# A planner that takes transfers to land later, early weight sums on GpSimd alone, half loads for unused half blocks, and another order of first-layer products

## The chip, the cores and the metric

The kernel runs on one core of a Trainium2 chip. The metric is the time of one execution on the device in microseconds (us), the median of several executions. The engines of the core are TensorE (PE in the profile; its weight loads are PEld), VectorE (DVE), ScalarE (ACT), GpSimd (POOL) and SyncE (SP, which issues the transfers). Matrix products are written to PSUM[...]; everything else lies in SBUF or in device memory.

## The reference

Two parts follow each other. The first is a state-space scan (batch 4, 8 heads, 768 steps, head size 32, state size 16, in chunks):

```python
L = np.exp(cum[:, :, :, None] - cum[:, :, None, :]) * causal
M = np.einsum('bhin,bhjn->bhij', Cc, Bc) * L
y = np.einsum('bhij,bhjd->bhid', M, xc) + np.einsum('bhin,bhnd->bhid', Cc, state) * np.exp(cum)[..., None]
state = decay_full[:, :, None, None] * state + np.sum(Bx, axis=2)
```

The second takes its result as x with 3,072 tokens of 256 numbers and runs four experts (256 to 1,024 to 256, all fp32), each weighted per token:

```python
p = domain_probs / (domain_probs.sum(-1, keepdims=True) + 1e-09)
for e in range(E):
    h = np.maximum(x @ w1[e], 0.0)
    out += p[:, e:e + 1] * (h @ w2[e])
```

## The kernel before

The tokens are 24 chunks of 128. They are taken in five blocks: three of four chunks (scheme `B`) and two of six (scheme `H`). For each block the scan of its chunks gives the tokens, and then both layers of all four experts are run on them. Each expert's 1,024 hidden columns are four blocks of 256 (`fb`), so there are 16 of them.

The products of a block are not made one by one. A scheme is a fast matrix multiplication: it forms sums of weight blocks and sums of token blocks, makes fewer products of 128 x 256 blocks, and recovers the wanted blocks from sums of the products. `B` takes 2 x 2 x 2 blocks with 7 products, `H` takes 3 x 2 x 3 blocks with 15. One call of `product` (line 831) is one such product. `Scheme.sums` lists the sums of weights, ten for `H` and four for `B` in each layer; `Scheme.blocks` says which blocks come straight from the weights. Blocks called "b" enter sums alone, and never a product by themselves.

`operands` loads the weights of one group into W tiles (32 of them, 128 x 512), makes the sums (line 942) into further W tiles and stores these in device memory (`w_d`, line 947). Where a group's sums are already stored, it loads them instead (line 939). For the `H` blocks, which come last, the sums are made early, during units 1 to 10, by `early_sums`, with a due time that lies a unit later. A unit is a step of the main loop: in scheme `B` two groups of two weight blocks, in scheme `H` one group of three. Its first-layer products (`twos_first`, `threes_first`) are interleaved by `put` with the second-layer products (`visit`) of the unit before.

In `threes_first`, `mul(r)` makes product r into a bank, `snap` copies a bank into a V tile (ScalarE, line 840), `seed` copies a V tile into a bank for further accumulation (ScalarE, line 845), `combine` adds or subtracts (VectorE or GpSimd, line 858), `gate` applies the rectifier and the expert's share (VectorE, line 866). `visit` copies its bank out on line 1111. The scan part has `mask` (ScalarE, line 437, from an xb tile), `scan` (VectorE, line 456), `fade` (GpSimd, line 462), the products of line 444 (scores), 469 and 775 (outputs), copies of the outputs (ScalarE, lines 791, 476 to 479), and `cts` (GpSimd, line 739).

The order of work on each engine is not written out by hand, except TensorE's: `Plan.run` is a list scheduler. Every piece of work has a price in us per engine it may run on, pieces that it needs, and the tiles that it touches. The scheduler walks through a modelled time and takes, for the engine that is free first, the ready piece with the earliest latest time (`latest`, counted back from its consumers or from a due time). TensorE takes its pieces in the given order. A transfer is modelled with a rate of 310 KB per us and fixed lags. A piece that needs the result of another may start `HOP` = 0.2 us after it, and a tile may be taken 0.2 us after its last use. Work with two engines in its price (`B256`, `B512`) goes to GpSimd only if that is in time and VectorE has a backlog. The resulting orders are then issued; on the chip each engine works through its own in order, held by semaphores.

`BY_DMA` is empty, so `sums_by_dma` is never called.

Of the kernel before, what the change touches and what calls it, by code (L numbers as in the profile page):

```python
# [10 lines left out]
ALU = mybir.AluOpType  # L11
# [7 lines left out]
HOP = 0.2  # L19
# [5 lines left out]
EARLY = 1, 2, 3, 4, 5, 6, 7, 8, 9, 10  # L25
SOFT = 1
ROUND = 0, 3, 2, 0, 4
RATE = 310.0
BY_DMA = ()
AFTER = 1  # L30
HELD = ("x", "w"), (5, 8), (0, 7)
LAST = (0, 1), (0, 2), (1, 1), (1, 2), (0, 0), (1, 0)
LATE = (13, 2), (6, 9), (11, 4), (10, 12), (3,), (1, 14), ("x", "w"), (5, 8), (0, 7)
ACC = 5.0
PAIRS_AT = {(3, 2): {0: 0, 1: 1}, (4, 2): {0: 0, 2: 1}, (4, 3): {0: 0, 1: 1, 2: 2},
            (6, 3): {0: 0, 2: 1, 3: 2}}


class Home:
    def __init__(self, tile_):  # L40
        self.tile, self.free, self.full = tile_, 0.0, False


class Value:
# [18 lines left out]
class Plan:  # L63
# [61 lines left out]
    def homed(self, w, at):  # L125

        taken, when = {}, at
        for v in w.touched:
            if v.home is not None:
                continue  # L130
            if w.reuse and w.reuse.left == 1 and w.reuse.kind == v.kind:
                taken[v] = w.reuse.home
                when = max(when, w.reuse.end)
                continue
            spare = [h for h in self.spare[v.kind] if h not in taken.values()]
            if v.seeded:
                spare = [h for h in spare if h.full]
            elif v.kind == "bank":
                hollow = [h for h in spare if not h.full and h.free <= at]
                spare = hollow or spare  # L140
            if not spare:
                return None, None
            if v.kind == "bank" and len(self.spare["bank"]) <= sum(
                    x.home is None and x.place < v.place for x in self.banks):
                return None, None
            if v.kind == "V" and len(spare) <= KEEP and w.latest + self.late > at + 8:
                return None, None
            if v.kind == "W" and len(spare) <= sum(
                    x.home is None and x.latest < v.latest for x in self.ws):
                return None, None  # L150
            h = min(spare, key=lambda h: h.free)
            taken[v] = h
            when = max(when, h.free + HOP)
        return when, taken

    def backlog(self, queue, now, free, but):
# [8 lines left out]
    def run(self, line, at, begin):  # L165
# [18 lines left out]
        while todo:  # L184
# [4 lines left out]
            for w in waiting[e]:  # L189
                if w.start is not None or e == "PE" and w.place != head:  # L190
                    continue
                ready = max([w.ready, w.after.nominal + late if w.after else 0.0] + [
                    n.end + (0.0 if n.by == e and e != "SP" else HOP) for n in w.needs])
                if len(w.on) > 1 and e == "POOL":
                    if max(ready, now) + w.on[e] > w.latest + late + SLACK or self.backlog(
                            waiting["DVE"], now, t["DVE"], w) < BACK:
                        continue
                rank = w.latest
                if e == "DVE" and w.two and self.port > now + 0.05:
                    rank += YIELD  # L200
                if best is not None and ready <= now and rank >= best[0]:
                    continue
                when, homes = self.homed(
                    w, max(now, ready, self.port if e == "POOL" and w.port else 0.0))
                if when is None:
                    continue
                if when <= now + 0.02:
                    if best is None or rank < best[0]:
                        if e == "DVE" and w.two:
                            when = max(when, self.port)  # L210
                        best = rank, w, when, homes
                elif soon is None or when < soon:
                    soon = when
# [30 lines left out]
            for v in w.touched:  # L244
                v.left -= 1
                v.end = max(v.end, w.end)
                if v.left == 0 and not (w.reuse is v and any(
                        x.home is v.home for x in w.touched if x is not v)):
                    v.home.free, v.home.full = v.end, v.fills
                    self.spare[v.kind].append(v.home)  # L250
# [58 lines left out]
def kernel(  # L309
# [55 lines left out]
    def some(n, shape, name, pool=const):  # L365
# [16 lines left out]
        "M": some(6, [HN, NQ, D], "M"),  # L382
        "gate": some(3, [P, max(b.n for b in blocks), P], "gate"),
        "Y": some(12, [P, FB], "Y"),
        "dram": [None] * 200,
    }
    st = {c: {} for c in range(NCH)}
    one = nc.const_aps.tensor(1.0, [P, 1])
# [495 lines left out]
            return w1[e, i * P:i * P + P, f * FB:f * FB + FB]  # L884
        return w2[e, f * FB:f * FB + FB, i * P:i * P + P].rearrange("(j p) m -> p j m", p=P)

    def sums_by_dma(scheme, fbs, l, after, due):

        slot = {}
        for i, pair in enumerate(scheme.shared[l]):  # L890
            d = stored_sums((*fbs, l, i))
            for j, r in enumerate(pair):
                slot[r] = d[:, j * FB:j * FB + FB]
        sums = {}
        for n, (r, x, y, sign) in enumerate(scheme.sums):
            if x not in scheme.blocks[l]:
                x, y = y, x
            f, i = scheme.blocks[l][x]
            v = sums[r] = value("dram")
            split = (lambda t: t) if l == 1 else (lambda t: t.rearrange("p (j m) -> p j m", j=JJ))  # L900
            dma(lambda e, r=r, f=f, i=i: nc.sync.dma_start(
                out=split(slot[r]), in_=source(fbs[f], l, i)), 1, 300, writes=[v], due=due, after=after)
            if y in sums:
                plan.add({"POOL": 1.0}, lambda e, r=r, y=y: nc.gpsimd.dma_start(
                    out=slot[r], in_=slot[y], accum_op=ALU.add), port=False, lag=ACC, kb=300,
                    reads=[sums[y]], part=[v], due=due, after=after)
            else:
                g, h = scheme.blocks[l][y]
                plan.add({"POOL": 1.0}, lambda e, r=r, g=g, h=h: nc.gpsimd.dma_start(
                    out=split(slot[r]), in_=source(fbs[g], l, h), accum_op=ALU.add), port=False, kb=300,  # L910
                    lag=ACC, part=[v], due=due, after=after, reads=[v])

    def operands(k, scheme, fbs, l, after=None, due=None):

        load, half = ((load_w1, w1_half), (load_w2, w2_half))[l - 1]
        where = {}
        for f, fb in enumerate(fbs):
            v = value("W")
            if l == 1 and f == 1 and (*fbs, l, 0) in w_d:
                dma(lambda e, v=v, fb=fb: nc.sync.dma_start(  # L920
                    out=v.t[:, FB:], in_=w1_rows(fb, 1)), kb=128, part=[v], after=after)
            else:
                dma(lambda e, v=v, fb=fb: load(fb, v.t), part=[v], after=after)
            for r, x in scheme.blocks[l].items():
                if x[0] == f:
                    where[r] = v, x[1]
# [10 lines left out]
        if keys[0] in w_d:  # L937
            for key, v in zip(keys, shared):
                dma(lambda e, v=v, key=key: nc.sync.dma_start(out=v.t, in_=w_d[key]), part=[v])
        else:  # L940
            for r, x, y, sign in scheme.sums:
                plan.add(B256, lambda e, r=r, x=x, y=y, sign=sign: (  # L942
                    on(e).tensor_add if sign > 0 else on(e).tensor_sub)(view(r), view(x), view(y)),
                    two=True, reads=[where[x][0], where[y][0]], part=[where[r][0]])
            for key, v in zip(keys, shared):
                d = stored_sums(key)
                dma(lambda e, v=v, d=d: nc.sync.dma_start(out=d, in_=v.t), reads=[v],
                    due=due or (lambda v=v: v.readers[-1]))
        weights[k, fbs, l] = where, view

    def early_sums(scheme, fbs, l, after, due):
        operands("early", scheme, fbs, l, after, due)

    def token_sums(k):
        Y, scheme = {}, blocks[k].scheme
# [72 lines left out]
    def threes_first(k, fbs):  # L1028
# [11 lines left out]
        mul(11, b7)  # L1040
        a12 = combine(b7, s12, -1)
        gate(2, 0, mul(0, seed(s7)))
        b6 = mul(6)
        t67 = combine(snap(b6), s7, -1)
        b3 = mul(3)
        s3 = snap(b3)
        b5 = mul(5, seed(a12))
        gate(2, 2, b5)
        mul(2, b7)
        gate(1, 2, combine(b7, s12, -1))  # L1050
        mul(10, b3)
        v = combine(b3, s12, -1)
        t67 = combine(t67, v)
        mul(14, b6)
        f = combine(b6, a12)
        f = combine(f, b5, -1)
        z02 = combine(f, s3, -1, reuse=s3)
        gate(0, 2, z02)
        mul(13, b7)
        gate(1, 0, b7)  # L1060
        b8 = mul(8, seed(v))
        gate(0, 1, b8)
        u = combine(f, b8, -1)
        gate(1, 1, mul(4, seed(v)))
        mul(1, b8)
        gate(2, 1, negate(t67, b8))
        gate(0, 0, mul(9, seed(u)))
        return seq, h
# [247 lines left out]
    for u, (k, groups) in enumerate(units):  # L1316
# [21 lines left out]
            leave(*ending, due=lambda n=u + AFTER: ends[min(n, len(ends) - 1)])  # L1338
            ending = None
        for _ in range(EARLY.count(u)):  # L1340
            (sums_by_dma if len(early) in BY_DMA else early_sums)(
                H, *early.pop(0), merged[0],
                lambda n=u + SOFT: ends[min(n, len(ends) - 1)])
        if groups is None:
            behind = second(k, *held, HELD if k == len(blocks) - 1 else (), plain)
        else:
# [80 lines left out]
```

## Time and profile before

| what | value |
|---|---|
| time, median of 3 runs | 635.5 us (634.72 to 637.93) |
| the profiled execution's own time | 636.7 us |
| its span (first to last instruction) | 634.9 us |
| granted TensorE clock | 0.998 |
| busy PE / DVE / ACT / POOL | 624.9 / 530.3 / 261.4 / 204.6 us |
| transfers on the main queue | 127.46 MB, 62.8% of 16 engines' span |
| full and half loads of raw weights (w<-in_w_dram) | 149 of 256 KB, 19 of 128 KB |
| sums of weights, line 942 | 80 on DVE, 84 on POOL |

A line of the timeline gives the start in us from the beginning of the span, the length in us, the engine, the line of the kernel, the operation, result and operands, the number of instructions merged, and in brackets the idle time of the engine just before and what ended it. A line of the waits gives who waited for whom, the total in us, how often, and the longest. DMA issues stand on SPq and are not counted as busy time of an engine; a semaphore event of a transfer is its landing.

### The profile page before, as it was taken

To read this page: it belongs to the slowest core of one execution; us is meant where nothing else is said; L and a number is where in the kernel's file an instruction comes from. 1 tells how busy PE (TensorE), PEld (TensorE's weight loads), DVE (VectorE), ACT (ScalarE), POOL (GpSimd) and SP (SyncE) were. 2 spreads that over 40 slices of the span, in tenths; PEclk is the share of its full clock that TensorE was granted. 3 is DMA by queue.
4 is the path that set the end of the run, shared out by engine and by line. 5 is a ranking of instruction groups with operands and counts; after the bars stand their busy time and mean duration, and the time that the engine had idled before them with its cause. 6 is when DMAs were issued, how large, how long until landed. Compare 5 with 4: busy or idle time off the path is not lost.

```text
span 634.9 us, 10197 instructions
## 1 busy us (share of the span) xinstructions
PE 624.9 (98%) x3363; PEld 528.7 (83%) x3363; DVE 530.3 (84%) x915; ACT 261.4 (41%) x538; POOL 204.6 (32%) x221
## 2 busy tenths in 40 slices
PE   9899999999998999999999999999999999999997
PEld 5687788888886888888888888888888888888886
DVE  7889987988968887888978887979897887779784
ACT  4123543434344253434434335455434235455441
POOL 4252533445422255442424614301053600101010
PEclk9999999999999999999999999999999999999999
DMA  6999794595899658489999928455232324951001
GB/s 202 287 303 362 234 323 160 175 299 141 275 322 341 233 172 268 107 256 305 326 349 363 305 40 294 150 154 174 77 91 83 101 45 120 377 167 56 2 1 51
DMA packets 110933, 128.37 MB, mean 202 GB/s; under 512 B 28692, under 2 KB 76832, under 8 KB 110880
## 3 DMA queue, kind: packets, MB, share of 16 engines
q1 hardware_dynamic: 110500, 127.46, 62.8%
q8 instruction: 27, 0.44, 0.3%
q10 hardware_dynamic: 380, 0.25, 0.1%
q14 instruction: 26, 0.21, 0.1%
HBM read 102.79 MB, written 24.89 MB: 201 GB/s over the span
## 4 chain that ended last, share of the span: by engine, by line
PE 51%; DVE 1%; issue 0%; DVEq 0%
PE bank L831 50%; PE bank L444 1%; PE bank L469 0%; DVE LT L456 0%; DVE v L866 0%; PE bank L775 0%; PE bank L1234 0%; DVE bank L1016 0%; DVE v L858 0%; DVE v L1162 0%; DVE v L1239 0%; DVE w L942 0%; DVEq L1239 0%
## 5 line engine op out<-in xcount | busy, mean ns | idle before, releaser
L831 PE MATMUL bank<-v,w 128*128 128x256 f32 x1864 | 441.6, 381 | 4.8 <-ACT A L479 2.4
L831 PEld LDWEIGHTS bank<-v,w 128*128 128x128 f32 x1864 | 351.2, 190 | 61.5 <-DVE v L866 5.4
L831 PE MATMUL bank<-Y,w 128*128 128x256 f32 x792 | 203.1, 379 | 0.1
L858 DVE TENSOR_TENSOR v<-v,v 128x512 f32<-128x512 f32 x216 | 161.9, 769 | 12.2 <-ACT v L840 8.1
L831 PEld LDWEIGHTS bank<-Y,w 128*128 128x128 f32 x792 | 150.2, 190 | 21.3 <-issue 0.7
L866 DVE SCALAR_TENSOR_TENSOR v<-bank,gate 128x512 f32<-128x512 f32 x172 | 116.7, 684 | 40.6 <-PE bank L831 33.5
L858 POOL TENSOR_TENSOR v<-v,v 128x512 f32<-128x512 f32 x54 | 79.7, 1480 | 214.1 <-DVE v L866 167.6
L1111 ACT COPY v<-bank 128x512 f32<-128x512 f32 x107 | 62.6, 585 | 157.6 <-PE bank L831 157.0
L845 ACT COPY bank<-v 128x512 f32<-128x512 f32 (+1 forms) x192 | 107.4, 577 | 33.0 <-DVE v L858 21.4
L840 ACT COPY v<-bank 128x512 f32<-128x512 f32 x106 | 62.0, 586 | 100.6 <-PE bank L831 87.4
L942 POOL TENSOR_TENSOR w<-w,w 128x256 f32<-128x256 f32 x69 | 58.1, 855 | 75.2 <-DMA w<-in_w_dram 23.6
L456 DVE TENSOR_TENSOR_SCAN LT<-ab,ident 128x512 f32<-128x512 f32 x42 | 54.3, 1311 | 3.7 <-DMA ab<-acut_d 3.7
L858 DVE TENSOR_TENSOR v<-bank,v 128x512 f32<-128x512 f32 x40 | 27.4, 685 | 11.8 <-PE bank L831 11.5
L942 DVE TENSOR_TENSOR w<-w,w 128x256 f32<-128x256 f32 x69 | 31.6, 487 | 6.3 <-DMA w_d<-w 3.8
L601 DVE TENSOR_TENSOR MT<-bank,LT 128x256 f32<-128x256 f32 x93 | 32.1, 410 | 0.2
L739 POOL TENSOR_TENSOR cts<-ctm,dec 128x256 f32<-128x256 f32 x20 | 17.1, 865 | 43.0 <-DVE dec L736 32.1
L437 ACT ACTIVATE ctm<-xb,tmask 128x128 f32<-128x128 f32 x48 | 16.0, 394 | 36.1 <-DMA xb<-in_xbc_dram 18.1
L1162 POOL TENSOR_TENSOR v<-v,v 128x256 f32<-128x256 f32 x22 | 18.9, 875 | 34.0 <-ACT v L1111 32.7
L462 POOL TENSOR_TENSOR MT<-xb,LT 128x128 f32<-128x128 f32 x20 | 11.5, 579 | 31.6 <-DVE LT L456 20.6
L1162 DVE TENSOR_TENSOR v<-v,v 128x256 f32<-128x256 f32 x38 | 17.2, 482 | 3.0 <-ACT v L1111 2.7
L942 POOL TENSOR_TENSOR w<-w 128x256 f32<-128x256 f32 x15 | 13.2, 885 | 16.3 <-DMA w<-in_w_dram 14.8
L1016 DVE TENSOR_TENSOR bank<-bank,v 128x512 f32<-128x512 f32 x22 | 15.2, 690 | 1.8 <-PE bank L831 1.8
(76 smaller groups left out, 210.5 us busy)
## 6 DMA issues: line engine op xcount, KB each, us to landing
w<-in_w_dram SPq DMA_DIRECT2D x149, 256.0 KB
w<-w_d SPq DMA_DIRECT2D x130, 256.0 KB
w_d<-w SPq DMA_DIRECT2D x82, 256.0 KB
ab<-acut_d SPq DMA_DIRECT2D x21, 512.0 KB
xb<-in_xbc_dram SPq DMA_DIRECT2D x12, 320.0 KB
gate<-p_d SPq DMA_DIRECT2D x10, 384.0 KB
gate<-p_d SPq DMA_DIRECT2D x11, 256.0 KB
w<-in_w_dram SPq DMA_DIRECT2D x19, 128.0 KB
```

Source lines behind the costliest of these rows:

```text
L437: nc.scalar.mul(ctm[:, t], xb[:, OCT:OCT + P], tmask[:, t:t + 1])
L456: nc.vector.tensor_tensor_scan(out=LT.rearrange("p h s -> p (h s)")[:, lo:lo + w], data0=src, data1=ident.rearrange("p h s -> p (h s)")[:, ...
L601: nc.vector.tensor_mul(MT[:, h, 0:P], g, LT[:, h])
L739: plan.add({"POOL": .78}, lambda e: nc.gpsimd.tensor_mul(s["cts"].t, s["ctm"].t, s["dec"].t.unsqueeze(1).to_broadcast([HN, NT, P])), reads ...
L831: nc.tensor.matmul(out=o, lhsT=w[:, j], rhs=x if half is None else x[:, j], start=(start and j == 0), stop=(j == 1), skip_group_check=True)
L840: act(.6, lambda e: nc.scalar.copy(out=flat(v), in_=bank.t), reads=[bank], writes=[v])
L845: act(.6 if to > FB else .38, lambda e: nc.scalar.copy(out=bank.t[:, :to], in_=flat(v)[:, :to]), reads=[v], writes=[bank])
L858: plan.add(engines, lambda e: (on(e).tensor_add if sign > 0 else on(e).tensor_sub)(flat(v), whole(x), whole(y)), reads=[x, y], writes=[v], ...
L866: dve(.7 if x.kind == "bank" else .74, lambda e: nc.vector.scalar_tensor_tensor(out=h.t, in0=whole(x).rearrange("p (j m) -> p j m", j=JJ), ...
L942: plan.add(B256, lambda e, r=r, x=x, y=y, sign=sign: (on(e).tensor_add if sign > 0 else on(e).tensor_sub)(view(r), view(x), view(y)), two= ...
L1111: act(.6, lambda e: nc.scalar.copy(out=flat(v), in_=bank.t), reads=[bank], writes=[v])
L1162: plan.add(engines, lambda e: (on(e).tensor_add if sign > 0 else on(e).tensor_sub)(o[1](), x[1](), y[1]()), reads=[v for v in vs if v is n ...
```

## The change

Five things are altered. A constant `MARGIN` of 4.0 us takes the place of `HOP` where a piece that does not run on SP needs the result of a transfer, and where such a piece takes a tile that was last touched by a transfer. The sums with a due time, which are the early ones, may run on GpSimd alone. `operands` loads only the used half of a weight tile where exactly one of its two blocks enters a product and the sums are stored already; before, it did so for the first layer's second tile only. `threes_first` makes its products in another order. The unused code of sums by transfers goes, and `operands` is called directly.

```diff
-RATE = 310.0
-BY_DMA = ()
+RATE, MARGIN = 310.0, 4.0
...
-        self.tile, self.free, self.full = tile_, 0.0, False
+        self.tile, self.free, self.full, self.dma = tile_, 0.0, False, False
...
-            when = max(when, h.free + HOP)
+            when = max(when, h.free + (MARGIN if h.dma and "SP" not in w.on else HOP))
...
-                    n.end + (0.0 if n.by == e and e != "SP" else HOP) for n in w.needs])
+                    n.end + (MARGIN if n.kb and e != "SP" else 0.0 if n.by == e and not n.kb else HOP)
+                    for n in w.needs])
...
             for v in w.touched:
                 v.left -= 1
                 v.end = max(v.end, w.end)
+                v.home.dma = w.kb > 0 if w.end == v.end else v.home.dma
...
-            if l == 1 and f == 1 and (*fbs, l, 0) in w_d:
-                dma(lambda e, v=v, fb=fb: nc.sync.dma_start(
-                    out=v.t[:, FB:], in_=w1_rows(fb, 1)), kb=128, part=[v], after=after)
+            used = {x[1] for r, x in scheme.blocks[l].items() if x[0] == f and r != "b"}
+            if len(used) == 1 and (*fbs, l, 0) in w_d:
+                i, = used
+                dma(lambda e, v=v, fb=fb, i=i: nc.sync.dma_start(
+                    out=half(v.t, i), in_=source(fb, l, i).rearrange(
+                        "p (j f) -> p j f", j=JJ) if l == 1 else source(fb, l, i)),
+                    kb=128, part=[v], after=after)
...
-                plan.add(B256, lambda e, r=r, x=x, y=y, sign=sign: (
+                plan.add({"POOL": .78} if due else B256, lambda e, r=r, x=x, y=y, sign=sign: (
...
         gate(2, 0, mul(0, seed(s7)))
-        b6 = mul(6)
-        t67 = combine(snap(b6), s7, -1)
         b3 = mul(3)
         s3 = snap(b3)
         b5 = mul(5, seed(a12))
         gate(2, 2, b5)
+        mul(10, b3)
+        v = combine(b3, s12, -1)
+        b6 = mul(6)
+        t67 = combine(snap(b6), s7, -1)
         mul(2, b7)
         gate(1, 2, combine(b7, s12, -1))
-        mul(10, b3)
-        v = combine(b3, s12, -1)
-        t67 = combine(t67, v)
         mul(14, b6)
...
         gate(0, 2, z02)
-        mul(13, b7)
-        gate(1, 0, b7)
+        gate(1, 1, mul(4, seed(v)))
         b8 = mul(8, seed(v))
         gate(0, 1, b8)
         u = combine(f, b8, -1)
-        gate(1, 1, mul(4, seed(v)))
+        mul(13, b7)
+        gate(1, 0, b7)
         mul(1, b8)
+        t67 = combine(t67, v)
         gate(2, 1, negate(t67, b8))
         gate(0, 0, mul(9, seed(u)))
...
-            (sums_by_dma if len(early) in BY_DMA else early_sums)(
-                H, *early.pop(0), merged[0],
-                lambda n=u + SOFT: ends[min(n, len(ends) - 1)])
+            operands("early", H, *early.pop(0), merged[0],
+                     lambda n=u + SOFT: ends[min(n, len(ends) - 1)])
```

More of the change, by code (lines that the diff above doesn't have):

```diff
@@ L33 @@
 LATE = (13, 2), (6, 9), (11, 4), (10, 12), (3,), (1, 14), ("x", "w"), (5, 8), (0, 7)
-ACC = 5.0
 PAIRS_AT = {(3, 2): {0: 0, 1: 1}, (4, 2): {0: 0, 2: 1}, (4, 3): {0: 0, 1: 1, 2: 2},
@@ L384 @@
         "Y": some(12, [P, FB], "Y"),
-        "dram": [None] * 200,
     }
@@ L885, in source @@
         return w2[e, f * FB:f * FB + FB, i * P:i * P + P].rearrange("(j p) m -> p j m", p=P)
[L887 to L911, printed above, removed]
     def operands(k, scheme, fbs, l, after=None, due=None):
@@ L949, in operands @@
         weights[k, fbs, l] = where, view
-    def early_sums(scheme, fbs, l, after, due):
-        operands("early", scheme, fbs, l, after, due)
     def token_sums(k):
```

## The prediction

> **What bounds the kernel now.** I read the page first, then the waits of TensorE, then the timeline around each of them. On the page, the busy line and the slices:
>
> ```profile
> PE 624.9 (98%) x3363; PEld 528.7 (83%) x3363; DVE 530.3 (84%) x915; ACT 261.4 (41%) x538; POOL 204.6 (32%) x221
> ...
> PE   9899999999998999999999999999999999999997
> ...
> DMA  6999794595899658489999928455232324951001
> ```
>
> TensorE is busy 624.9 of 634.9 us, and the chain that ended last is nearly all L831. The number of products (`product`, L831) does not change, so the change can win only what TensorE stands still: 10.0 us, of which the ends (a start-up that is not planned, 1.1 us, and the last copy and store, 3.7 us) are out of reach. The dips are in slices 2 and 13. From the waits of PE:
>
> ```profile
> PE bank L831 <- ACT A L479: 2.4, 1, 2.4
> PE bank L831 <- DVE v L866: 2.0, 2, 1.2
> ...
> PE bank L831 <- DVE v L858: 0.4, 2, 0.2
> ```
>
> Five waits, 4.8 us. The timeline shows how the largest came about:
>
> ```profile
> 18.64 0.71 PE L444 MATMUL bank<-ctm,xb 32*128 32x256 f32 x8
> ...
> 22.56 0.69 ACT L437 ACTIVATE ctm<-xb,tmask 128x128 f32<-128x128 f32 x2 [7.72 <-DMA xb<-in_xbc_dram]
> ...
> 23.16 0.35 ACT L791 COPY v<-bank 128x256 f32<-128x256 f32 x1
> 23.41 0.18 ACT L479 COPY A<-bank 128x32 f32<-128x32 f32 x1
> ...
> 23.64 1.99 PE L831 MATMUL bank<-v,w 128*128 128x256 f32 x8 [2.37 <-ACT A L479]
> ```
>
> ScalarE stood 7.7 us at `mask` (L437), whose xb had not landed. Behind it in ScalarE's order stood the copies that empty a bank (L791, L479); their matmuls were over at 18.7. TensorE wanted that bank and waited 2.4 us. The planner had believed the transfer landed earlier. The second place:
>
> ```profile
> 188.03 0.42 DVE L942 TENSOR_TENSOR w<-w,w 128x256 f32<-128x256 f32 x1 [2.90 <-DMA w_d<-w]
> ...
> 192.36 1.99 PE L831 MATMUL bank<-v,w 128*128 128x256 f32 x8 [1.24 <-DVE v L866]
> 193.25 1.22 DVE L942 TENSOR_TENSOR w<-w,w 128x256 f32<-128x256 f32 x3 [0.94 <-DMA w_d<-w]
> ...
> 195.13 4.58 PE L831 MATMUL bank<-v,w 128*128 128x256 f32 x20 [0.77 <-DVE v L866]
> ...
> 199.88 1.13 PE L831 MATMUL bank<-v,w 128*128 128x256 f32 x4 [0.17 <-DVE v L858]
> ```
>
> Here VectorE stood 2.9 and 0.9 us at an early sum of weights (L942), because the W tile it was to write was still being stored (w_d<-w). The gatings (L866) and sums (L858) queued behind came late, and TensorE waited 1.24 + 0.77 + 0.17 = 2.18 us.
>
> [...] In the trace L858 with a PSUM input takes 685 ns, from SBUF alone 769 on average; L942 on VectorE takes 406 ns at least and up to 1,472. [...] the trace has 855 against 487 ns.
>
> **The change part by part.**
>
> 1. *Later landings (MARGIN 4.0 instead of HOP 0.2).* No instruction is added or taken away; the order on ACT, DVE, POOL and SP changes, TensorE's does not through this part. Anything that reads a transfer, or writes a tile last touched by one, is placed 3.8 us later in the plan. At 23.64, the mask goes behind L791 and L479, which can then run from 18.7 on: 2.4 us of idle go (2.8 by the weight loads' own idle time). What is late next there is VectorE: its L601 ends at 22.1, before TensorE would reach outputs([3]) at some 22.7, so no new wait. At 67.18 ScalarE waits 5.83 us in the same way; TensorE's weight load loses 0.5 us at 68.46, and I count 0.3. Sum of this part: 2.7 us. Behind the new delays stand `scores` (needs ctm), `cts` and `fade` on POOL (need xb, ah). The tightest `cts` of the trace starts at 172.8 for an L775 at 179.6, 6.1 us ahead after its 0.73; the others are 12 to 24 us ahead. 3.8 us later fits. Where TensorE in the plan now has to wait for weights, its real order stays, but filler may get in front of work it needs: one filler is 0.7 to 1.2 us (L858, L456).
>
> 2. *Early sums on GpSimd alone.* There are 100 (5 groups, 2 layers, 10 sums). The line's view from 136 us on, where only these are left:
>
> ```profile
> L942 POOL TENSOR_TENSOR w<-w,w x41: 718/735/1639, 135.9 to 334.9; 128x256 f32<-128x256 f32 x41
> L942 DVE TENSOR_TENSOR w<-w,w x31: 407/417/1472, 151.4 to 337.1; 128x256 f32<-128x256 f32 x31
> ```
>
> With the other form (w<-w) VectorE makes 35 there, POOL 46. Moved: 35 x 0.487 = 17 us less on VectorE, 35 x 0.855 = 30 us more on POOL over 200 us, where POOL is about a third busy: it has the room. VectorE then never stands at the store of a W tile: the 2.18 us of 192 to 200 go, and I count 1.9, as gatings there also had L456 scans of 1.2 us ahead of them. POOL still meets such waits (4.3 us at 177.83), with `fade`, `cts` and some L858 queued behind. [...] At 306.91 (0.23 us idle) VectorE also had sums ahead: 0.2.
>
> 3. *Half blocks.* Layer 1 already loads half of group block 1. New are halves for layer 2 (block 0 of scheme B, block 1 of scheme H). If these are as many as the 19 halves of now, 19 x 131 KB = 2.5 MB of 128 MB go, 2%; at 62.8% of 634.9 us for 127.46 MB that is 8 us of the 16 engines' time. TensorE waits for no weights beyond 0.3 us, so it is worth nothing directly: a transfer hidden anyway. It makes landings slightly earlier; from 0 to 0.5 us, I take 0. Issues stay the same number. Their rows are 512 bytes instead of 1,024[...].
>
> 4. *Order in `threes_first`.* Ten units, all from some 340 us on, where no wait of TensorE is seen at all: nothing to win. What can it cost? Products alternate with second-layer ones, 0.86 us apart in the timeline. Product 14 now comes two places after 6: three products less, 2.6 us, for the copy of bank b6 (L840: in the unit at 447.81 it ended 0.8 us after its product; the worst near it 1.1). Product 5 comes one place earlier after 11: 4.3 us for L858 (0.69) and L845 (0.59), which in that unit were over 2.7 us after the product (445.2 to 447.9). Product 13 comes two places later: its gating (0.69) has 3.5 us before the next house uses it. All fit, so 0; if half of the ten units lost 0.5 us it would be 2.5 us.
>
> *Sum.* Gain 2.7 + 1.9 + 0.2 = 4.8 us. Against it I set 0.6 us of new small waits from the reshuffled order (the trace of before cannot show them; bounds: nothing, or five fillers of 1 us). Net 4.2 us. Against the profiled execution: 636.7 (span 634.9, 1.8 around it) - 4.2 = 632.5. That execution lies 1.2 above the median 635.5, so the forecast for the median is 635.5 - 4.2 = **631.3 us**. The floor, all reachable idle time gone with the weight loads' share of it, is 6.5 less: 629.0.
>
> **The rivals.**
>
> *Same time, chance 0.27.* The order is a list-schedule of 10,000 instructions; removing the two stalls moves everything, and stalls of the same kind return elsewhere: VectorE stays 80% busy and keeps one W store or scan too many ahead of a gating. For it: VectorE is the releaser of four of five waits[...]. Against it: both large waits have a transfer behind them. With half of 4.8 us back and the reordering at its worst 1 us: 635.5 - 1.4 = 634.1. I set its bounds at 3.2 us either way, which is 0.5%, about what a measurement of this kernel can tell from no change.
>
> *Slower, chance 0.18: GpSimd's queue becomes the bound at the pair boundaries.* Early sums no longer pass to VectorE when POOL is late, and POOL runs in order. It has waited up to 11.2 us for the load of weights and 6.2 us for TensorE to free a W tile in L942. If such a wait stands ahead of `fade` or `cts` of a pair, L775/L469 come late and TensorE stands. It decides where the wait exceeds the lead, 6.1 us at the tightest: (11.2 - 6.1) = 5.1 us for one. Two of these among the boundaries cost 10.2, against 4.8 won: 635.5 + 5.4 = 640.9. Against it: the other leads are 12 us and more, and later planned landings put sums behind their loads.
>
> *It does not do what it says.* MARGIN could leave the mask before L791 if the plan had the landing later than that anyway. Then 1.9 us stay: 633.6, inside the same-time case.
>
> **How the numbers follow.** Faster as worked out 0.55, same 0.27, slower 0.18. Range: below, the floor of 629.0; above, half of the slower case, 639.5, as the small-cost bounds (5 us of fillers, 2.5 us of the new order) end at 638.2 and one long POOL wait alone ends near 636. The likeliest case's own range is 629.0 to 632.3.
>
> **What would show it.** Right: no wait of PE over 0.5 us near 23 and 192; ACT L437 idle on xb gone or with nothing behind it; L942 on DVE down from 80 to about 35 to 45 and on POOL up to about 120 to 130; POOL's busy time up some 30 us to about 235, DVE's down some 15; half loads about 38 and full loads about 130; the last stretch from 340 us without waits. Wrong: PE waits on L739 or L462 work (POOL), on L840 or L845 between 340 and 625, or on DMA w<-in_w_dram; or slices 2 and 13 still below 9.

## The result, and the profile after

The changed kernel takes 630.62 us (median of 6 executions, 628.9 to 632.63), the kernel before in the same comparison 637.7 us (6 executions, 634.72 to 638.95; the first three alone gave the 635.5 that the prediction started from). The ratio is 0.990, interval 0.987 to 0.993: 1% faster, which is 6.4 us of 637.7; the two medians lie 7.1 us apart. The profiled execution took 630.59 us, its span is 628.8 us against 634.9.

The page of the changed kernel, its busy line and two of the slices:

```profile
PE 622.6 (99%) x3363; PEld 529.3 (84%) x3363; DVE 526.0 (84%) x869; ACT 261.9 (42%) x538; POOL 254.3 (40%) x267
...
PE   9999999999999999999999999999999999999997
...
DMA  7999795484898965699997827546123333951001
```

TensorE has the same 3,363 instructions and is busy in every slice; slices 2 and 13 no longer dip. GpSimd is busy 49.7 us more than before, VectorE only 4.3 us less. The waits of PE (lines have moved: 831 is now 830, 840 is 839, 942 is 919):

```profile
PE bank L830 <- ACT v L839: 1.2, 2, 0.7
PE bank L603 <- PEq L1392: 0.8, 1, 0.8
PE bank L443 <- ACT p_sb L567: 0.3, 1, 0.3
PE bank L468 <- DVE MT L600: 0.2, 1, 0.2
```

The 2.4 us behind L479, and the 2.4 us behind VectorE's L866 and L858, are gone; 1.2 us behind L839 (a `snap`) are new. The timeline at the place of the first stall:

```profile
17.49 0.93 PE L468 MATMUL bank<-MT,xb 128*32 128x144 f32 x16 [0.15 <-DVE MT L600]
...
18.48 0.37 ACT L790 COPY v<-bank 128x256 f32<-128x256 f32 x1 [3.94 <-PE bank L468]
18.75 0.19 ACT L478 COPY A<-bank 128x32 f32<-128x32 f32 x1
...
19.00 3.72 PE L830 MATMUL bank<-v,w 128*128 128x256 f32 x16
...
21.96 1.40 ACT L436 ACTIVATE ctm<-xb,tmask 128x128 f32<-128x128 f32 x4 [3.02 <-DMA xb<-in_xbc_dram]
```

The masks now stand behind the copies of the bank, and two products follow each other without a gap at 19.00. The masks still wait 3.0 us for xb, but nothing is queued behind them that TensorE wants. At the second place VectorE no longer makes early sums; of the early sums GpSimd makes all, and one of them still meets a store, where it costs nothing:

```profile
POOL w L919 <- DMA w_d<-w: 4.8, 1, 4.8
```

The next timeline is that of the changed kernel at the second place. The products run on without a wait:

```profile
187.19 7.93 PE L830 MATMUL bank<-v,w 128*128 128x256 f32 x36
```

Where the time came from can be read by setting the n-th matmul of one trace beside the n-th of the other. The changed kernel is 0.3 us ahead from the start-up, 2.8 us ahead after the place near 23 us, 2.2 after 42.6 (a wait of its own), 2.7 after 68, 5.8 after 200, 5.2 after 275.9 (the second wait of its own) and 6.1 us ahead at the end. The times of its own waits are those of its trace, the others those of the trace before.

### The profile page after: what moved, and what is told of

It is laid out like the page before. It is cut to its first block, busy times and chain, and to the rows that moved or that the text cites. A ratio compares the mean times of both kernels' runs of the same rounds, so it can differ in the third digit from the quotient of the medians.

```text
span 628.8 us, 10190 instructions
## 1 busy us (share of the span) xinstructions
PE 622.6 (99%) x3363; PEld 529.3 (84%) x3363; DVE 526.0 (84%) x869; ACT 261.9 (42%) x538; POOL 254.3 (40%) x267
## 3 DMA queue, kind: packets, MB, share of 16 engines
q1 hardware_dynamic: 110500, 124.97, 62.3%
## 4 chain that ended last, share of the span: by engine, by line
PE 93%; DMA 3%; DVE 2%; ACT 1%; issue 0%; SPq 0%; POOL 0%; ACTq 0%; POOLq 0%; DVEq 0%
PE bank L830 87%; PE bank L468 2%; DMA ab<-acut_d 2%; PE bank L443 2%; DMA w<-in_w_dram 1%; PE bank L774 1%; PE bank L603 1%; PE bank L580 0%; DVE LT L455 0%; DVE v L857 0%; DVE v L865 0%; POOL v L857 0%; DVE MT L600 0%; SPq L418 0%; DVE w L919 0%
## 5 line engine op out<-in xcount | busy, mean ns | idle before, releaser
L857 POOL TENSOR_TENSOR v<-v,v 128x512 f32<-128x512 f32 x71 | 101.0, 1424 | 190.4 <-DVE v L857 84.4
L857 DVE TENSOR_TENSOR v<-v,v 128x512 f32<-128x512 f32 x199 | 162.8, 841 | 17.9 <-ACT v L839 14.5
L919 POOL TENSOR_TENSOR w<-w,w 128x256 f32<-128x256 f32 x102 | 89.9, 901 | 40.3 <-PE bank L830 29.6
L839 ACT COPY v<-bank 128x512 f32<-128x512 f32 x106 | 61.9, 585 | 100.7 <-PE bank L830 97.7
L857 DVE TENSOR_TENSOR v<-bank,v 128x512 f32<-128x512 f32 x40 | 27.6, 689 | 17.6 <-PE bank L830 16.4
L738 POOL TENSOR_TENSOR cts<-ctm,dec 128x256 f32<-128x256 f32 x20 | 19.1, 965 | 43.5 <-DVE dec L735 20.8
L1136 POOL TENSOR_TENSOR v<-v,v 128x256 f32<-128x256 f32 x20 | 17.1, 865 | 45.2 <-ACT v L1085 45.1
L1136 DVE TENSOR_TENSOR v<-v,v 128x256 f32<-128x256 f32 x40 | 18.6, 493 | 4.6 <-ACT v L1085 4.3
L919 DVE TENSOR_TENSOR w<-w,w 128x256 f32<-128x256 f32 x36 | 17.4, 506 | 0.2
L919 POOL TENSOR_TENSOR w<-w 128x256 f32<-128x256 f32 x13 | 10.2, 790 | 17.4 <-DMA w<-in_w_dram 15.8
```

Of the source, the lines that this page charges most:

```text
L738: plan.add({"POOL": .78}, lambda e: nc.gpsimd.tensor_mul(s["cts"].t, s["ctm"].t, s["dec"].t.unsqueeze(1).to_broadcast([HN, NT, P])), reads ...
L839: act(.6, lambda e: nc.scalar.copy(out=flat(v), in_=bank.t), reads=[bank], writes=[v])
L857: plan.add(engines, lambda e: (on(e).tensor_add if sign > 0 else on(e).tensor_sub)(flat(v), whole(x), whole(y)), reads=[x, y], writes=[v], ...
L919: plan.add({"POOL": .78} if due else B256, lambda e, r=r, x=x, y=y, sign=sign: (on(e).tensor_add if sign > 0 else on(e).tensor_sub)(view(r ...
L1136: plan.add(engines, lambda e: (on(e).tensor_add if sign > 0 else on(e).tensor_sub)(o[1](), x[1](), y[1]()), reads=[v for v in vs if v is n ...
```

## The experiments

The theory on trial: two transfers landed later than the planner believed (its planned times are not on record; that it put the waiting instructions first says so); in each case an in-order queue stood still at the instruction that needed the transfer, and work for TensorE stood behind it. The rival: the gain comes from the plan as a whole, or from a less loaded VectorE. The first group leaves the plan of the kernel before as it is and edits single pieces after planning. The second runs parts of the change.

**b_mask**, the wrong mask, and so a check of the noise:

```diff
...
+    done.remove(st[4]["masked"])
+    done.insert(done.index(st[2]["keep"]) + 1, st[4]["masked"])
     for w in done:
         w.fn(w.by)
```

> The kernel before, planned as it was; after planning, one piece is moved: ScalarE's mask of chunk 4 goes behind the copies that empty the bank of chunk 2. Theory (a late transfer at the head of an in-order queue): the wait of TensorE near 23.6 us goes, nothing else moves; span 634.9 less 2.5 to 2.8 = 632.1 to 632.4, the wait near 192 us stays at 2.2 us or more. Rival (TensorE is short of something else there, the gating or the next bank): a wait of over 1 us returns within the next 10 us and the span stays within 1 us of 634.9.

Measured: ratio 0.9997 (0.9982 to 1.0012), span 636.0. The order on every engine was that of the kernel before: it is chunk 5's mask, which needs three transfers (L395 to L397), that stood ahead of the copies, and chunk 4's was behind them already. The wait near 24 us stayed, at 3.25 us in this run. So the run decides nothing on the theory, but shows that a comparison of equal kernels comes out within 0.2%.

**b_mask5**, the same edit with the other mask:

```diff
...
+    done.remove(st[5]["masked"])
+    done.insert(done.index(st[2]["keep"]) + 1, st[5]["masked"])
```

> As b_mask, but it is the mask of chunk 5 that is moved behind the copies of chunk 2: in the trace the first of the two masks near 23 us follows the three transfers of a turned chunk, so it is chunk 5's, and chunk 4's, which b_mask moved, stood behind the copies already. Theory (a late transfer at the head of an in-order queue): the wait of TensorE near 23.6 us, 2.4 to 3.3 us, goes, and nothing else moves; ratio 0.9950 to 0.9965. Rival (TensorE is short of something else there): over 1 us of waiting returns within the next 10 us, ratio over 0.998.

Measured: ratio 0.9973 (0.9957 to 0.9989), 1.7 us instead of the 2.4 to 3.3. The wait near 24 us is gone, as the theory has it, but the gain is less than the theory's range. The rival is right in part: 15 us later other waits come up, and the waits of TensorE after the start-up, 6.5 us in b_mask, still add up to 5.0 us here. The timeline of b_mask5:

```profile
36.04 2.34 DVE L456 TENSOR_TENSOR_SCAN LT<-ab,ident 128x512 f32<-128x512 f32 x2 [3.32 <-DMA ab<-acut_d]
...
38.30 0.67 DVE L866 SCALAR_TENSOR_TENSOR v<-bank,gate 128x512 f32<-128x512 f32 x1
...
39.02 1.13 PE L831 MATMUL bank<-v,w 128*128 128x256 f32 x4 [1.24 <-DVE v L866]
```

A third late transfer, that of ab, holds a scan at the head of VectorE's queue; the gating behind it is late. In the kernel before, VectorE waited there too (3.0 us), but TensorE, late by its first stall, did not notice. The next cause was the same kind of cause.

**b_five**, five sums after planning:

```diff
...
+    sums = [w for w in done if getattr(w, "sum", False) and w.by == "DVE"]
+    for w in sums[54:59]:
...
+        w.by = "POOL"
     for w in done:
         w.fn(w.by)
```

> The kernel before, planned as it was; after planning, five early sums (those that VectorE runs from 188 to 195 us) are issued on GpSimd instead, at their places in the order. Theory (the store of a W tile holds VectorE's queue): the waits of TensorE at 192, 195 and 200 us go or fall under 0.5 us in all; span less 2.5 to 3.1, so 631.8 to 632.4; the wait at 23.6 stays. Rival (VectorE is simply too full there, with scans and gatings): five times 0.49 us less VectorE work gives at most about 1 us of the 3, the waits stay at 1.5 us or more.

Measured: ratio 0.9953 (0.993 to 0.9977), 3.0 us. The waits near 192, 195 and 200 us are gone. The waits of PE in b_five:

```profile
PE bank L831 <- ACT A L479: 3.2, 1, 3.2
PE bank L604 <- PEq L1424: 0.8, 1, 0.8
PE bank L444 <- ACT p_sb L568: 0.4, 1, 0.4
PE bank L469 <- DVE MT L601: 0.2, 1, 0.2
```

In the kernel before these five instructions were some 2 us of VectorE's work and 3.8 us of waiting for stores; moving them gave 3.0 us of the whole time. GpSimd took over waits for stores (11.0 us in all, 6.6 before) without TensorE noticing. The rival of a merely too full VectorE isn't excluded by this alone: the 1 us that it was allowed is an estimate, and the interval reaches down to 1.5 us. What excludes it is e_margin below, where VectorE is busier than before and these waits are gone all the same.

**b_both** was to be both edits, with the wrong mask, and so repeats b_five:

> The kernel before with both edits after planning: the one mask moved, the five sums on GpSimd. Theory: the two effects add, span 634.9 less 5.0 to 5.9 = 629.0 to 629.9, within 1 us of the changed kernel's 628.8 without a new plan, half loads or another order of products; ratio to before about 0.991. Rival (the changed kernel's gain needs its new plan as a whole): less than 3 us of gain.

Measured: ratio 0.9937 (0.9915 to 0.996), with the wait behind L479 still there, 4.3 us. It says nothing on whether the effects add. **b_both5** bears on that, with chunk 5's mask:

> The kernel before, planned as it was, with both edits after planning: chunk 5's mask moved, the five early sums on GpSimd. Theory: the two effects add to 5.5 to 6.5 us, ratio 0.990 to 0.9915, no wait of TensorE over 1 us: as fast as the changed kernel without a new plan. Rival (the changed kernel's gain needs its plan as a whole): ratio over 0.9935.

Measured: ratio 0.9927 (0.9898 to 0.9956), 4.7 us, between the two readings, and its interval reaches into both. It is what the two measured alone make together (0.9973 x 0.9953 = 0.9926), so the effects add as far as this can tell. In the trace the stalls near 24 and 192 are both gone; what is missing to the changed kernel is the scan at ab again, now with 4.30 us of waiting, and 2.26 us of TensorE behind it. The products after that wait ran at a granted clock of 0.50 (41.00 to 44.41 us), which cost another 1.5 us (last section).

**e_margin**, the later landings alone, in the plan:

```diff
...
-                    n.end + (0.0 if n.by == e and e != "SP" else HOP) for n in w.needs])
+                    n.end + (MARGIN if n.kb and e != "SP" else 0.0 if n.by == e and not n.kb else HOP)
+                    for n in w.needs])
...
```

(and the same for tiles last touched by a transfer)

> The kernel before with the later landings alone (MARGIN 4.0 in both places of the planner). Theory: the wait near 23.6 us goes (2.5 to 2.8 us). VectorE's sums are also planned behind the stores of their tiles, so most of the 2.2 to 3.0 us near 192 go as well: span 629.5 to 632.4. Rival (later landings only reshuffle): the wait near 23.6 goes but waits of VectorE's gatings turn up elsewhere, span 633 or more.

Measured: ratio 0.9893 (0.9864 to 0.9923), span 630.0. The whole gain of the change, from one constant. Between the start-up and 400 us no wait of TensorE over 0.2 us is left, and none behind the scan at ab; and VectorE never waits for a store, although it makes 102 of the 164 sums here, 22 more than in the kernel before, and is busy 541.1 us instead of 530.3. So it was the waiting for stores that held TensorE near 192, not the amount of VectorE's work. What is left is 1.4 us near 409, 422 and 426 us:

```profile
PE bank L834 <- ACT bank L848: 1.4, 3, 0.6
```

**e_pool**, the early sums on GpSimd alone, in the plan:

```diff
-                plan.add(B256, lambda e, r=r, x=x, y=y, sign=sign: (
+                plan.add({"POOL": .78} if due else B256, lambda e, r=r, x=x, y=y, sign=sign: (
```

> The kernel before with the early sums on GpSimd alone, in the plan. Theory: the wait near 192 us goes (about 3 us), the wait near 23.6 stays since no early sum lies there: ratio 0.995 to 0.997. Rival (GpSimd's queue takes over the wait): gratings of TensorE's waits on POOL-fed work appear and the ratio is over 0.998.

Measured: ratio 0.9988 (0.997 to 1.0006), no gain. The stall near 192 is gone, but the new plan made another of the first kind. The timeline of e_pool:

```profile
283.50 1.27 ACT L437 ACTIVATE ctm<-xb,tmask 128x128 f32<-128x128 f32 x4 [7.31 <-DMA xb<-in_xbc_dram]
...
284.68 1.04 ACT L840 COPY v<-bank 128x512 f32<-128x512 f32 x2
285.29 1.13 PE L831 MATMUL bank<-Y,w 128*128 128x256 f32 x4 [3.89 <-ACT v L840]
```

ScalarE stands 7.3 us at two masks, with two `snap` copies behind them, and TensorE loses 3.9 us. It is not GpSimd's queue that took over the wait, as that rival had it, but a mask, as at 23.6. The wait near 24 us is there too, with 3.5 us, and after it the granted clock was 0.50 from 25.2 to 28.6 us and 0.96 on average from 30 to 40 us (last section).

**a_nomargin**, the changed kernel without the later landings:

```diff
...
-            when = max(when, h.free + (MARGIN if h.dma and "SP" not in w.on else HOP))
+            when = max(when, h.free + HOP)
...
-                    n.end + (MARGIN if n.kb and e != "SP" else 0.0 if n.by == e and not n.kb else HOP)
-                    for n in w.needs])
+                    n.end + (0.0 if n.by == e and e != "SP" else HOP) for n in w.needs])
...
```

> The changed kernel with the old 0.2 us in both places of the planner; the early sums on GpSimd, half loads and the new order stay. Theory: the wait near 23.6 us is back (2.4 to 3.6 us), that near 192 is not; ratio to before about 0.995, so the changed kernel's landings are worth half of its gain. Rival (later landings are worth nothing once the sums are on GpSimd): ratio 0.99.

Measured: ratio 0.9974 (0.9952 to 0.9995). The wait behind L479 is back with 3.1 us, and one of 3.2 us behind a `snap` near 283 us, the same as in e_pool. Of the changed kernel's gain some 1.7 us are left without the landings, so they are worth more than the half that was expected.

**after_same**, **margin_order**, **a_nohalf** and **a_m8** share their runs of the kernel before:

> The changed kernel once more, to be compared with the next three under the same runs of the kernel before. Both theories: ratio 0.987 to 0.993; TensorE's waits between first and last product 1.5 to 2.5 us by the gaps between products.

Measured: 0.9909 (0.9876 to 0.9941), median 630.93, span 628.8.

margin_order is e_margin with the eight moved lines of `threes_first` as well, as in the diff of the change:

```diff
...
-        b6 = mul(6)
-        t67 = combine(snap(b6), s7, -1)
         b3 = mul(3)
...
+        b6 = mul(6)
+        t67 = combine(snap(b6), s7, -1)
...
```

> The kernel before with the later landings and the new order of products; early sums stay free to go to either engine, no further half loads. Theory (later landings do it all; the other parts are worth under 1 us): within 0.3% of the changed kernel. The waits of 0.5 to 0.7 us near 409, 422 and 426 us that the later landings alone showed go if the order is what removes them. Rival (the sums on GpSimd are needed to keep VectorE clear near 192): a wait of over 1 us near 190 and a ratio 0.3% or more above the changed kernel's.

Measured: 0.9904 (0.9885 to 0.9923), median 631.38. Within the 0.3%, and no wait near 190. The small waits near 409 stay (0.8 us in two), so the order isn't what removes them.

a_nohalf undoes the new half loads in the changed kernel:

```diff
-            if len(used) == 1 and (*fbs, l, 0) in w_d:
...
+            if l == 1 and f == 1 and (*fbs, l, 0) in w_d:
...
```

> The changed kernel with half loads in the first layer alone, as before: 2.5 MB more are moved. Theory (a transfer that is hidden anyway): within 0.3% of the changed kernel. Rival (the full transfers slow the landings that queues wait for): 0.3% or more slower than it, with waits of TensorE behind masks or scans.

Measured: 0.9898 (0.9875 to 0.992), median 630.72. The same as the changed kernel. Its profiled execution shows two waits behind a `snap`, 2.8 us in all, at the two places where the changed kernel has 1.2, and took 632.72, the longest of its four.

a_m8 has a margin twice as long:

```diff
-RATE, MARGIN = 310.0, 4.0
+RATE, MARGIN = 310.0, 8.0
```

> The changed kernel with MARGIN 8.0 in place of 4.0. In its trace the two waits left over 0.5 us, near 42.6 and 275.9, again have a mask that stands at a late xb ahead of the copies of a bank. Theory (the margin is still too short for those): both go, span down by up to 1.5 us, at most 0.25%. Rival (too long a margin puts masks and scans so late that scores or gatings come late): new waits, ratio above that of the changed kernel.

Measured: 0.9874 (0.9854 to 0.9894), median 629.79, span 628.0. Both waits went. The waits of PE in a_m8:

```profile
PE bank L603 <- PEq L1392: 0.8, 1, 0.8
PE bank L443 <- ACT p_sb L567: 0.4, 1, 0.4
PE bank L830 <- ACT bank L844: 0.3, 1, 0.3
```

It is the fastest version run, 1.1 us below the changed kernel by the medians; the intervals of the two ratios overlap, so that much is not shown. Only 0.3 us of its TensorE waits lie after the start-up.

## Why the prediction was right, and where not

It forecast 631.3 us, 4.2 us less than the 635.5 it started from; measured are 630.62 and a gain of 6 to 7 us. Sign and mechanism hold, and the time lies in the range. That the time was met so closely is in part luck: the kernel before has 637.7 by six executions, 2.2 us above the 635.5 of the first three, and 4.2 less than 637.7 would be 633.5. A start that was too low and a gain that was too small made up for each other. By its own steps:

- *The bound.* That only time in which TensorE stands still can be won holds: its instructions did not change at all, and 6.1 us of span are less than the 10.0. Its idle time fell by 3.8 us, its busy time by 2.3. A part of the latter is waiting too: at 23.64 the start of the next product moved by 2.53 us where the wait is given as 2.37, and the waits at 192 to 200 each have the same 0.16 us on top.
- *Part 1, 2.7 us for the later landings: mis-sized, because it was credited with half of its work.* The part alone is worth 0.9893, all of the gain. The prediction saw that tiles touched by a transfer are also planned later, but counted the stores at 192 under part 2. The step "What is late next there is VectorE ... so no new wait" came true by a cause that it didn't name: with the mask alone out of the way (b_mask5) a scan that waits for ab costs TensorE 1.2 us at 39 us, and a gating at 43 another 0.7; it is the later landing of ab, in the same part, that removes these (e_margin). The view of the kernel before had the scan, as a 3.0 us wait of VectorE; it was passed over as it released nothing of TensorE's then.
- *Part 2, 1.9 us for GpSimd alone: the stall was read rightly, the part not.* b_five shows that taking those sums off VectorE is worth 3.0 us where nothing else moves. But as a rule of the plan it gives nothing by itself (e_pool, 0.9988), as the new plan put masks ahead of copies again and left those near 24 us where they were, and beside the later landings it isn't needed (margin_order, 0.9904 against 0.9909). The sums of weights on VectorE fell from 80 to 49, not to 35 to 45, and rose on GpSimd to 115, not to 120 to 130. The relief forecast for VectorE, some 15 us by the author's estimate, was 4.3: it issues fewer instructions (869 instead of 915), but its sums from SBUF take 841 ns instead of 769. In the trace 83 of these 199 sums overlap with an instruction of GpSimd and take 1,058 ns on average, the other 116 take 686; before, 63 of 216 overlapped. Sums with an input from PSUM (v<-bank,v) take 688 ns with an overlap and 691 without. Why the overlapping sums from SBUF take longer was not shown. GpSimd's rise was 49.7 us, not 30: 28.8 are sums of weights (100.1 instead of 71.3), and 21.3 are 17 more of the sums of L858, now L857 (71 instead of 54).

```profile
L857 POOL TENSOR_TENSOR v<-v,v 128x512 f32<-128x512 f32 x71 | 101.0, 1424 | 190.4 <-DVE v L857 84.4
L857 DVE TENSOR_TENSOR v<-v,v 128x512 f32<-128x512 f32 x199 | 162.8, 841 | 17.9 <-ACT v L839 14.5
```

- *Part 3, nothing for the half loads: right.* 130 full and 38 half loads, 124.97 MB instead of 127.46, and no difference in the time (a_nohalf). The time of the 16 engines on the main queue fell by 7.0 us where 8 were estimated (62.3% of 628.8 us instead of 62.8% of 634.9).
- *Part 4, nothing for the order: right* by margin_order beside e_margin (0.9904 and 0.9893, their intervals overlap). The waits near 409 us appear in both and not in the changed kernel. Which of the other parts moves them was not separated; they are about 1 us.
- *New small waits, 0.6 us:* the changed kernel has 1.2 us, at 42.6 and 275.9. Both are masks ahead of a `snap` that wait for xb; with a margin of 8 us both waits are gone (a_m8).
- *The rivals.* The slower case, GpSimd's queue, did not occur: it waits 56 us at L919 in all, and no wait of TensorE ends with it. "Same time, because stalls of the same kind return elsewhere" is what e_pool did, where the later landings were missing.

The 4.2 was too small by about 2 us. By the matmuls set side by side, 192 to 200 gave some 3.0 us instead of 1.9, the places near 307 and 325 some 0.7 instead of 0.2, and the start-up 0.3; the new waits took 1.1 instead of 0.6. The start-up is not an effect of the change: the first product starts between 12.5 and 13.2 us in the traces of these kernels.

## What to carry to other kernels

Where engines work through fixed orders, look for the instruction that waits longest for a transfer and read what stands behind it in its queue: what counts is not how long it waits but whom it blocks. Where a planner's landing times are too early, such places can be many: here removing one by hand uncovered the next (b_mask5), while a margin on all of them gave the whole 1% at once. A wait that is harmless now, because another engine is late anyway, belongs in the sum once that lateness is taken away.

## What the runs showed of the hardware that was not expected

In b_five a stall of TensorE cost more than its own length. The wait near 24 us, 3.17 us long, is followed by a stretch at a granted clock of 0.50, and the eight matmuls there take 3.6 us where the kernel before, at 23.64 us, took 2.0:

```profile
23.90 3.60 PE L831 MATMUL bank<-v,w 128*128 128x256 f32 x8 [3.17 <-ACT A L479]
```

b_mask had a wait of 3.25 us at the same place and stayed at a granted clock of 1.00: its next eight matmuls took 1.99 us. In e_pool, after 3.9 us at 285 us, the next four took 1.13 us, as four did in the kernel before at 199.88 us; after its 3.5 us near 24 us the clock was 0.50. The windows view (stretch; length, then busy us and, in brackets, instructions of PE, PEld, DVE, ACT and POOL; granted clock; share of the transfers and GB/s) shows a stretch behind the wait near 24 us of b_five, of e_pool and of b_mask, and one behind b_both5's wait of 2.26 us at 40.06:

```profile
24.12:27.53 3.41, 3.41 (x12) 2.23 (x15) 0.00 (x0) 0.32 (x2) 1.89 (x3) 0.50 0.96 281
...
25.20:28.60 3.40, 3.40 (x8) 2.29 (x8) 0.00 (x0) 0.30 (x2) 1.24 (x2) 0.50 0.93 328
...
24.70:28.20 3.50, 3.50 (x29) 2.69 (x30) 1.12 (x2) 1.23 (x5) 1.77 (x3) 1.00 0.86 282
...
41.00:44.41 3.41, 3.41 (x20) 2.24 (x20) 3.41 (x7) 1.39 (x4) 3.33 (x6) 0.50 0.91 338
```

The length of a wait alone does not decide: after b_both5's 2.26 us the clock was 0.50, after b_mask's 3.25 us it was 1.00. What decides was not shown.

Stretches at a lower granted clock are likely part of why the kernel before varies more from run to run (634.7 to 644.1 us over all comparisons) than the changed one (628.9 to 634.8), though no run tested it by itself: in the comparisons with experiments, its 19 executions with a mean clock of 0.995 or less have a median of 640.2 us, the 11 with 1.000 one of 638.0. The gain itself is not of this kind, as those 11 are still some 7 us slower than the changed kernel.
